# Paired heads in a cached-attention decode step, and a re-split of the last weight transfer

## The chip, the cores and the metric

The kernel runs on one core of one Trainium2 chip. Its five engines are TensorE (PE, matrix products), VectorE (DVE), ScalarE (ACT), GpSimd (POOL) and SyncE (SP, which here only issues DMAs). Sixteen DMA engines move data between device memory and the core's SBUF, whose 128 rows are called partitions. Matrix products land in PSUM, which DVE and ACT read. The metric is device time in microseconds of one execution, where smaller is better.

## The reference

One decode step for a batch of 4 tokens, model width 640, 32 heads of width 192. Attention looks at the last 2048 of 8192 cached positions. A gated feed-forward of width 1536 runs on the same normalised input, and the two results are added to the input.

```python
W = min(4096, max(256, Sk // 4))                 # 2048
q = (xn @ wq).reshape(B, Sq, Hq, Dh).transpose(0, 2, 1, 3)
scores = einsum("bhqd,bhkd->bhqk", q, k_cache[:, :, Sk - W:]) * Dh ** -0.5
o = einsum("bhqk,bhkd->bhqd", softmax(scores), v_cache[:, :, Sk - W:])
A = o.transpose(0, 2, 1, 3).reshape(B, Sq, Hq * Dh) @ wo
B = (silu(xn @ w1) * (xn @ w3)) @ w2
out = x + A + B                                   # xn = layernorm(x)
```

Nearly all bytes are the two caches: 32 heads x 3 MiB of keys and as much of values, all in bfloat16.

## The kernel before

A head's keys lie in SBUF as 128 partitions x 64 positions x 192: partition 4q+b holds 64 consecutive positions of batch row b. Values lie the same way, so no transposes of the caches are needed, and softmax over a batch row runs along 64 columns and across 32 partitions.

**Scores.** `mult` (L216) multiplies a chunk of `CH` = 16 positions of keys on DVE by the head's query, which `q_bcast` (L207) has spread over all partitions. `adder` (L225) sums the 192 products down to `DD` = 32 by six identity matmuls that accumulate in PSUM. `reduce_tile` (L233) sums those 32 on DVE. There are `NC` = 4 such steps per head, and 128 in all.

**Softmax.** `chain_lmax`, `chain_tr`, `chain_gmax`, `chain_bc` (L243 to L272) take each row's maximum: a DVE maximum, a PE transpose, a DVE maximum over 32 partitions, and a matmul that spreads it back. `chain_bc` then runs four exponentials on ACT per head, one for each batch row, each with a bias that sends the partitions of the other batch rows to zero. Their results are written straight into the columns of the weight tile `z`.

**Values.** `pv` (L281) multiplies `z` (32 columns, of which 8 are used: two positions x four batch rows) by two positions of values at a time: 32 matmuls of 384 columns per head, spread over four groups of PE columns. An ACT copy `o_sb` and `fold` (L297, a 32-bit selection matmul) gather the result. DVE scales it by the reciprocal row sum into `o_bf`. Every four heads `ge_tr` and `ge_proj` (L308, L315) transpose that and multiply by the output weights into `acc`.

**Tail.** `ffn_mm` (L338) forms the gate and up products, `ffn_transpose` (L356) turns their product around, and the loop at L417 multiplies by the down weights `w2`. Those are loaded in four transfers (L331): two whole thirds, three quarters of the last third, and its last quarter. The sum is added to `t1` and stored by two small DMAs.

**Order.** A table `sched` (L362 to L404) assigns every step a slot and a phase within it. One slot is one `mult`. Engines run their instructions in the order in which the steps are emitted, except where the Tile framework's scheduler reorders within the dependencies; `reduce_tile` is pinned on DVE behind the multiply `RLAG` slots ahead. All large loads are issued by SP in one order: keys of head h, values of head h-2, and so on. `kpool` and `vpool` hold three heads each, so keys of head h+3 wait until head h has been multiplied, and values of head h+3 until `pv` of head h is done. Eight DMA semaphores are used in turn, so a transfer is also issued no earlier than the landing of the one eight before it. The weights `w1`, `w3` and `w2` take over buffers of `kpool` at the end.

Of the kernel before, what the change touches and what calls it, by code (L numbers as in the profile page):

```python
# [18 lines left out]
def kernel(  # L19
# [12 lines left out]
    DD: int = 32,  # L32
    CH: int = 16,
    HG: int = 4,
    QP: int = 2,
    KBUFS: int = 3,
    VBUFS: int = 3,
    PBUFS: int = 4,
    NZ: int = 3,
    L: int = 9,  # L40
    RLAG: int = 2,
    ALIGN: int = 128,
):

# [3 lines left out]
    P = 128  # L48
# [12 lines left out]
    NS = H * NC  # L61
    RPP = (HG * Dh) // P
    QW = QP * Dh
    OW = HG * Dh
    NCH = 512
    FC = F // P
    DH = D // 2
    assert NJ % CH == 0 and CH * DD <= 512 and QW <= 512 and CH % 2 == 0
    assert (HG * Dh) % P == 0 and Dh % RPP == 0 and H % HG == 0 and HG % QP == 0
# [3 lines left out]
    NB = H // QP // NG  # L73
    assert H % (QP * NG) == 0 and NB <= 4
    assert DH <= 512 and F % NCH == 0 and NF <= NG and (NJ // 2) % NG == 0 and 2 * B <= 32
# [10 lines left out]
    ps_o = ctx.enter_context(tc.tile_pool(name="ps_o", bufs=2, space=MemoryType.PSUM))  # L86
# [4 lines left out]
    qbcs, wos, o_pss, rss, rcps, o_sbs, o_bfs, chs = ({} for _ in range(8))  # L91
    mult_insts = {}
# [5 lines left out]
    def load_k(h):  # L98
        kt = kpool.tile([P, NJ, Dh], BF16, tag="kt")
        nc.sync.dma_start(out=kt[:], in_=cache_rows(A_k_cache, h))  # L100
        kts[h] = kt

    def load_v(h):
        vt = vpool.tile([P, NJ, Dh], BF16, tag="vt")
        nc.sync.dma_start(out=vt[:], in_=cache_rows(A_v_cache, h))
        vts[h] = vt
# [6 lines left out]
    x_sb = const.tile([B, D], BF16, name="x_sb")  # L113
# [24 lines left out]
    ones_f = const.tile([P, 1 + ALIGN // 4], FP32, name="ones_f")[:, 0:1]  # L138
    nc.vector.memset(ones_f[:], 1.0)
    nsc = const.tile([1, B], FP32, name="nsc")  # L140
    nc.vector.memset(nsc[:], -SCALE)

    zs = []
    for i in range(NZ):
        z = const.tile([P, NJ // 2, 32], BF16, name=f"z{i}")
        nc.gpsimd.memset(z[:], 0.0)
        zs.append(z)
# [5 lines left out]
    rowsel = const.tile([P, 2 * B], FP32, name="rowsel")  # L153
    nc.vector.tensor_reduce(out=rowsel[:], in_=idf[:].rearrange("p (g c) -> p c g", g=NG)[:, 0:2 * B, :], axis=AX.X, op=ALU.add)
# [9 lines left out]
    sq = ppool.tile([B, D], FP32, tag="pr")  # L164
    ssq = const.tile([B, 1], FP32, name="ssq")
    nc.scalar.activation(out=sq[:], in_=xc[:], func=ACTF.Square, accum_out=ssq[:])
# [6 lines left out]
    xn = const.tile([B, D], BF16, name="xn")  # L173
# [10 lines left out]
    nc.vector.tensor_copy(out=sel[:], in_=rowsel[:, 0:B].unsqueeze(1).to_broadcast([P, NQ, B]))  # L184
    selT = ps_t.tile([P, B], FP32, tag="t")
    nc.tensor.matmul(selT[:], lhsT=sel[0:B].rearrange("k q b -> k (q b)"), rhs=idb[0:B, 0:B], start=True, stop=True)
    mbias = const.tile([P, B], FP32, name="mbias")
    nc.vector.tensor_scalar(out=mbias[:], in0=selT[:], scalar1=-1.0, scalar2=-MASK, op0=ALU.add, op1=ALU.mult)
# [4 lines left out]
    for k in range(NB):  # L193
        pool, tag = ((ps_add, "ps"), (ps_o, "o_ps"))[k // 2]
        qp = pool.tile([P, QW], FP32, tag=tag)
        q_pss.append(qp)
# [7 lines left out]
    for k in range(NB):  # L204
        nc.scalar.copy(out=q_sb[:, k, :], in_=q_pss[k][:])

    def q_bcast(qg):  # L207
        k, g = qg // NG, qg % NG
        bp = ps_t.tile([P, QW], FP32, tag="t")
        nc.tensor.matmul(bp[:], lhsT=sel[32 * g:32 * g + B].rearrange("k q b -> k (q b)"),  # L210
                         rhs=q_sb[32 * g:32 * g + B, k, :], start=True, stop=True)
        qbc = qpool.tile([P, QP, Dh], BF16, tag="qbc")
        nc.scalar.copy(out=qbc[:].rearrange("p h d -> p (h d)"), in_=bp[:])  # L213
        qbcs[qg] = qbc

    def mult(s):  # L216
        h, c = s // NC, s % NC
        pr = ppool.tile([P, CH, Dh], BF16, tag="pr")
        mi = nc.vector.tensor_tensor(out=pr[:], in0=kts[h][:, c * CH:(c + 1) * CH, :],  # L219
                                     in1=qbcs[h // QP][:, h % QP, :].unsqueeze(1).to_broadcast([P, CH, Dh]),  # L220
# [11 lines left out]

    def reduce_tile(s):  # L233
        h, c = s // NC, s % NC
        if c == 0:
            sc = small.tile([P, NJ], FP32, tag="sc", bufs=3)
            scs[h] = sc
        ri = nc.vector.tensor_reduce(out=scs[h][:, c * CH:(c + 1) * CH], in_=pss.pop(s)[:], axis=AX.X, op=ALU.add)  # L238
        ahead = min(s + RLAG, NS - 1)
        if ahead in mult_insts and ahead > s:  # L240
            tc.add_manual_dep(ri.ins, mult_insts[ahead].ins.name, ORDER_DEP, reason="vector engine issue order")

    def chain_lmax(h):  # L243
        lmax = small.tile([P, 1], FP32, tag="lmax")
        nc.vector.tensor_reduce(out=lmax[:], in_=scs[h][:], axis=AX.X, op=ALU.max)  # L245
        chs[h] = [lmax]

    def chain_tr(h):
        mt = ps_t.tile([P, P + B], FP32, tag="t")
        nc.tensor.transpose(out=mt[0:1, 0:P], in_=chs[h][0][:], identity=idf[:])  # L250
        chs[h].append(mt)

    def chain_gmax(h):
        gmax = small.tile([1, B], FP32, tag="gmax")
        nc.vector.tensor_reduce(out=gmax[:], in_=chs[h][1][0:1, 0:P].rearrange("o (q b) -> o b q", b=B),
                                axis=AX.X, op=ALU.max)
        gmq = small.tile([1, NQ, B], FP32, tag="gmq", bufs=1)
        nc.vector.tensor_copy(out=gmq[:], in_=gmax[:].unsqueeze(1).to_broadcast([1, NQ, B]))  # L258
        chs[h].append(gmq)

    def chain_bc(h):
        lmax, mt, gmq = chs.pop(h)
        sc = scs.pop(h)
        nc.tensor.matmul(mt[:, P:P + B], lhsT=gmq[:].rearrange("o q b -> o (q b)"), rhs=nsc[:], start=True, stop=True)  # L264
        negm = small.tile([P, B], FP32, tag="negm")
        nc.vector.tensor_tensor(out=negm[:], in0=mt[:, P:P + B], in1=mbias[:], op=ALU.add)  # L266
        z = zs[h % NZ][:].rearrange("p j (s b) -> p j s b", b=B)
        rs = small.tile([P, B], FP32, tag="rs")
        for b in range(B):
            nc.scalar.activation(out=z[:, :, 0:2, b], in_=sc[:].rearrange("p (j s) -> p j s", s=2), func=ACTF.Exp,  # L270
                                 bias=negm[:, b:b + 1], scale=SCALE, accum_out=rs[:, b:b + 1])
        rss[h] = rs  # L272

    def rowsum(h):
        tb = ps_t.tile([B, 1], FP32, tag="t")
        nc.tensor.matmul(tb[:], lhsT=rss.pop(h)[:], rhs=ones_f[:], start=True, stop=True)  # L276
        rcp = small.tile([B, 1], FP32, tag="rcp")
        nc.vector.reciprocal(out=rcp[:], in_=tb[:])  # L278
        rcps[h] = rcp

    def pv(s):  # L281
        h, c = s // NC, s % NC
        if c == 0:
            o_ps = ps_o.tile([P, 2 * Dh], FP32, tag="o_ps")
# [172 lines left out]
```

## Time and profile before

| | us |
|---|---|
| median of three runs | 529.87 (528.54 to 530.36) |
| the profiled execution: its own time | 528.51 |
| the profiled execution: its span | 526.6 |
| mean clock granted to TensorE in it | 0.853 of full |

In the profile, "busy" is the time an engine spent in instructions and "idle" names what it waited for. PEld is the loading of matmul weights, which overlaps PE. The DMA row gives the share of the sixteen engines' time that was spent moving packets. A completion of a DMA is written by each engine that took part in it, as a 4-byte packet behind its last data packet; the trace keeps the time, queue and size of each packet, but not the engine. Times within the execution are counted from the start of the span.

### The profile page before, as it was taken

Reading aid. Unit: us, or ns where it says so; the run is one execution under the profiler, and the core shown is the slowest. Engines: PE = TensorE matmul, PEld = TensorE weight load, DVE = VectorE, ACT = ScalarE, POOL = GpSimd, SP = SyncE. Lnnn points to the kernel's source line nnn. Section 1 sums busy time; section 2 is a strip of 40 time slices with the busy share of each in tenths; the row PEclk is TensorE's granted clock in tenths of the full one; section 3 lists DMA queues with packets and bytes.
Section 4 is the critical chain, followed back from the end, with each engine's and each line's share of the span. In section 5 each row is a group of like instructions: output and inputs, shape, how many; then the busy total and the mean of one; then the engine's idle time right before and its main releaser. Section 6 shows DMA issues by size and latency. Waiting matters only on the chain.

```text
span 526.6 us, 5872 instructions
## 1 busy us (share of the span) xinstructions
PE 360.0 (68%) x2384; PEld 148.4 (28%) x2384; DVE 340.2 (65%) x475; ACT 76.4 (15%) x318; POOL 4.5 (1%) x14
## 2 busy tenths in 40 slices
PE   1356767886676778767567976767678766668755
PEld 1122222332222333232222322223233322223322
DVE  4069766677666557777556677666567775665802
ACT  2101211101111111101111011111111011111130
POOL 3000000000000000000000000000000000000000
PEclk9999988778788887887878787888887887888888
DMA  8999999999999999999999999999999999999995
GB/s 359 439 425 437 429 429 431 432 424 435 437 429 435 429 434 429 433 432 431 429 433 428 426 440 426 437 429 431 432 433 431 429 436 430 431 426 440 423 426 218
DMA packets 11730, 223.33 MB, mean 424 GB/s; under 512 B 1316, under 2 KB 1464, under 8 KB 2872
## 3 DMA queue, kind: packets, MB, share of 16 engines
q1 hardware_dynamic: 11688, 222.97, 98.7%
q8 instruction: 18, 0.29, 0.2%
q14 instruction: 8, 0.07, 0.0%
q10 hardware_dynamic: 16, 0.01, 0.0%
HBM read 222.96 MB, written 0.01 MB: 423 GB/s over the span
## 4 chain that ended last, share of the span: by engine, by line
DMA 66%; DVE 21%; PE 9%; ACT 2%; issue 2%; SPq 0%; DVEq 0%; ACTq 0%
DMA kt<-in_A_k_cache_dram 61%; DVE pr L219 15%; PE ps L229 6%; DMA w2t<-in_B_w_dram 5%; DVE sc L238 5%; PE o_ps L289 1%; ACT z L270 1%; PE acc L321 1%; ACT o_sb L293 0%; DVE lmax L245 0%; SPq L129 0%; PE gp L312 0%; PE tb L276 0%; DVE rcp L278 0%; SPq L335 0%
## 5 line engine op out<-in xcount | busy, mean ns | idle before, releaser
L229 PE MATMUL ps<-pr,idb 128*128 128x512 bf16 x768 | 241.0, 470 | 110.4 <-DVE sc L238 101.1
L219 DVE TENSOR_TENSOR pr<-kt,qbc 128x3072 bf16<-128x3072 bf16 x128 | 223.3, 1745 | 35.5 <-DMA kt<-in_A_k_cache_dram 35.4
L229 PEld LDWEIGHTS <-idb 128*128 128x128 bf16 x768 | 85.3, 115 | 240.0 <-issue 190.4
L238 DVE TENSOR_REDUCE sc<-ps 128x16 f32<-128x512 f32 x128 | 86.9, 679 | 0.9 <-PE ps L229 0.9
L293 ACT COPY o_sb<-o_ps 128x384 f32<-128x384 f32 x32 | 15.1, 472 | 306.5 <-PE o_ps L289 306.5
L289 PE MATMUL o_ps<-vt,z 128*32 128x384 bf16 x1024 | 55.3, 334 | 3.8 <-DMA vt<-in_A_v_cache_dram 3.8
L270 ACT ACTIVATE z<-sc,negm 128x64 bf16<-128x64 f32 x128 | 45.7, 423 | 76.7 <-DVE negm L266 76.7
L266 DVE TENSOR_TENSOR negm<-mt,mbias 128x4 f32<-128x4 f32 x32 | 5.2, 161 | 70.7 <-PE mt L264 70.7
L306 DVE TENSOR_SCALAR o_bf<-fp,rcp 4x192 bf16<-4x192 f32 x32 | 12.9, 405 | 56.8 <-PE fp L302 29.9
L302 PE MATMUL fp<-o_sb,rowsel 128*4 128x192 f32 x128 | 26.7, 332 | 13.2 <-ACT o_sb L293 13.2
L289 PEld LDWEIGHTS <-z 128*32 128x32 bf16 x1024 | 25.0, 97 | 29.4 <-issue 20.8
L270 ACT ACTIVATION_READ_ACCUMULATOR z<-sc,negm 128x1 f32 x128 | 23.9, 187 | 0.0
L302 PEld LDWEIGHTS fp<-o_sb,rowsel 128*4 128x4 f32 x128 | 8.7, 87 | 24.2 <-ACT o_sb L293 18.6
L276 PE MATMUL tb<-ones_f,rs 128*4 128x1 f32 x64 | 6.2, 166 | 13.4 <-ACT z L270 13.4
L264 PE MATMUL mt<-nsc,gmq 1*128 1x4 f32 x64 | 12.2, 258 | 1.2 <-DVE gmq L258 1.2
L264 PEld LDWEIGHTS mt<-nsc,gmq 1*128 1x128 f32 x64 | 9.4, 183 | 12.1 <-issue 10.3
L276 PEld LDWEIGHTS tb<-ones_f,rs 128*4 128x4 f32 x64 | 3.6, 86 | 24.5 <-ACT z L270 23.0
L278 DVE RECIPROCAL rcp<-tb 4x1 f32<-4x1 f32 x32 | 4.9, 153 | 8.5 <-PE tb L276 8.5
L201 PE MATMUL qp<-wt,xnT 128*32 128x384 bf16 x80 | 7.0, 523 | 4.9 <-DMA wt<-in_A_wq_dram 4.9
L250 PE MATMUL mt<-idf,lmax 128*1 128x128 f32 x32 | 9.9, 308 | 0.5 <-DVE lmax L245 0.4
L321 PE MATMUL acc<-wt,oT 128*32 128x320 bf16 x96 | 9.7, 301 | 0.3 <-DVE oT L313 0.2
L213 ACT CAST qbc<-bp 128x384 bf16<-128x384 f32 x16 | 7.6, 485 | 7.7 <-PE bp L210 7.7
(61 smaller groups left out, 80.1 us busy)
## 6 DMA issues: line engine op xcount, KB each, us to landing
kt<-in_A_k_cache_dram SPq DMA_DIRECT2D x32, 3072.0 KB, 36.8
vt<-in_A_v_cache_dram SPq DMA_DIRECT2D x32, 3072.0 KB, 40.1
wt<-in_A_wo_dram SPq DMA_DIRECT2D x8, 960.0 KB, 36.5
wt<-in_A_wq_dram SPq DMA_DIRECT2D x2, 3072.0 KB, 13.2
wt<-in_B_w_dram SPq DMA_DIRECT2D x2, 1920.0 KB, 32.5
wt<-in_A_wq_dram SPq DMA_DIRECT2D x1, 1536.0 KB
w2t<-in_B_w_dram SPq DMA_DIRECT2D x2, 640.0 KB, 26.9
w2t<-in_B_w_dram SPq DMA_DIRECT2D x1, 480.0 KB, 27.6
```

The lines of the kernel that those rows point to most:

```text
L219: mi = nc.vector.tensor_tensor(out=pr[:], in0=kts[h][:, c * CH:(c + 1) * CH, :], in1=qbcs[h // QP][:, h % QP, :].unsqueeze(1).to_broadcast ...
L229: nc.tensor.matmul(ps[:], lhsT=idb[:], rhs=pr[:, :, kk * DD:(kk + 1) * DD], start=(kk == 0), stop=(kk == NK - 1))
L238: ri = nc.vector.tensor_reduce(out=scs[h][:, c * CH:(c + 1) * CH], in_=pss.pop(s)[:], axis=AX.X, op=ALU.add)
L250: nc.tensor.transpose(out=mt[0:1, 0:P], in_=chs[h][0][:], identity=idf[:])
L264: nc.tensor.matmul(mt[:, P:P + B], lhsT=gmq[:].rearrange("o q b -> o (q b)"), rhs=nsc[:], start=True, stop=True)
L270: nc.scalar.activation(out=z[:, :, 0:2, b], in_=sc[:].rearrange("p (j s) -> p j s", s=2), func=ACTF.Exp, bias=negm[:, b:b + 1], scale=SCAL ...
L276: nc.tensor.matmul(tb[:], lhsT=rss.pop(h)[:], rhs=ones_f[:], start=True, stop=True)
L289: nc.tensor.matmul(o_ps[32 * g:32 * g + 32, :], lhsT=z[:, jj, :], rhs=vt[:, 2 * jj:2 * jj + 2, :], start=(jj < NG), stop=(jj >= NJ // 2 - NG))
L293: nc.scalar.copy(out=o_sb[:].rearrange("r two d -> r (two d)"), in_=o_pss.pop(h)[:])
L302: nc.tensor.matmul(fp[:], lhsT=rowsel[:, two * B:(two + 1) * B], rhs=o_sb[:, two, :], start=(two == 0), stop=(two == 1))
L306: nc.vector.tensor_scalar_mul(out=o_bfs[hg][:, hl, :], in0=fp[:], scalar1=rcps.pop(h)[:, 0:1])
L321: nc.tensor.matmul(acc[32 * t:32 * t + 32, :], lhsT=oT[:, i, :], rhs=wo_t[:, i * D + t * DH:i * D + (t + 1) * DH], start=st, stop=sp)
```

## The change

The kernel works on two heads at a time (`HH` = 2) from the scores on, and on chunks of 32 positions (`CH` = 32, so `NC` = 2 steps per head; `DD` = 16, so twelve identity matmuls per step).

- The softmax chain runs once for two heads. One exponential per head, without masks, gives `e`; DVE multiplies it by the 0/1 mask `selb` into `z` (`chain_z`) for both heads.
- `pv` takes eight positions and 64 of the 192 value columns per matmul: 24 matmuls of 512 columns per head, on three groups of PE columns. Only the diagonal blocks of the result are wanted: `pick` multiplies by a 0/1 pattern on DVE, `pick_sum` adds up on DVE, `fold` gathers. PSUM output tiles are one pair deep (`ps_o` bufs 1) where there were two heads.
- The scaling by the reciprocal row sum moves from DVE to ACT, two calls per pair.
- Queries are projected in 60 matmuls of 512 columns (80 of 384 before), and broadcast in 12 pieces (16 before).
- In the schedule, values of head j are issued in the slot after head j's first multiply, and `pv` runs seven slots behind (a slot is now half a head).
- In the tail, the product of gate and up is formed twice: for all 512 columns, and once more (`hp`) for the columns of the last quarter of `w2`, in a permuted order. That quarter is loaded in two transfers (`w2_last`) of 64 partitions each, whose rows are read 8 by 8. `ffn_transpose` has a fifth transpose for it. The up product is now multiplied before `ge_tr`.

In the changed kernel PE runs the tail in this order: `pv` of the last head, `fold`, the up product, `ge_tr`, `ffn_transpose`, `ge_proj`, the down product. SP issues the same transfers in the same order as before, but for the first output weights, which go ahead of the fourth head's keys, and the two transfers in place of one at the end.

```diff
-    DD: int = 32,
-    CH: int = 16,
+    DD: int = 16,
+    CH: int = 32,
...
-    ps_o = ctx.enter_context(tc.tile_pool(name="ps_o", bufs=2, space=MemoryType.PSUM))
+    ps_o = ctx.enter_context(tc.tile_pool(name="ps_o", bufs=1, space=MemoryType.PSUM))
...
+        e = small.tile([P, HH, NJ], BF16, tag="e", bufs=2)
+        for hh in range(HH):
+            nc.scalar.activation(out=e[:, hh, :], in_=sc[:, hh, :], func=ACTF.Exp,
+                                 bias=negm[:, hh:hh + 1], scale=SCALE, accum_out=rs[:, hh:hh + 1])
...
+    def chain_z(u):
+        e = es.pop(u)
+        z = small.tile([P, HH, NJ, B], BF16, tag="z", bufs=2)
+        behind(nc.vector.tensor_tensor(out=z[:].rearrange("p h j b -> p (h j) b"),
+                                in0=e[:].rearrange("p h j -> p (h j)").unsqueeze(2).to_broadcast([P, HH * NJ, B]),
+                                in1=selb[:].unsqueeze(1).to_broadcast([P, HH * NJ, B]), op=ALU.mult))
...
+    def pv(j):
...
+        for g in range(GN):
+            for k in range(NV):
+                nc.tensor.matmul(o_ps[32 * k:32 * k + 32, hh, :],
+                                 lhsT=z[:, hh, g * PL:(g + 1) * PL, :].rearrange("p l b -> p (l b)"),
+                                 rhs=vt[:, g * PL:(g + 1) * PL, k * DV:(k + 1) * DV],
+                                 start=(g == 0), stop=(g == GN - 1))
+
+    def pick(u, h0, h1):
...
+        behind(nc.vector.tensor_tensor(out=o_ms[u][:, h0:h1].rearrange("r h l d -> r (h l) d"),
+                                       in0=o_pss[u][0:NV * 32, h0:h1, :].rearrange("r h (l d) -> r (h l) d", l=PL),
+                                       in1=diag[0:NV * 32, h0:h1, :].rearrange("r h l -> r (h l)").unsqueeze(2).to_broadcast([NV * 32, n, DV]), op=ALU.mult))
+
+    def pick_sum(u, h0, h1):
...
+        behind(nc.vector.tensor_reduce(out=o_rs[u][:, h0:h1, :], in_=o_ms[u][:, h0:h1].rearrange("r h l d -> r h d l"), axis=AX.X, op=ALU.add))
+
+    def fold(u):
...
+        for k in range(NV):
+            nc.tensor.matmul(fp[:, :, k * DV:(k + 1) * DV], lhsT=fsel[0:NV * 32, k, :], rhs=o_r[:], start=True, stop=True)
...
+        for hh in range(HH):
+            nc.scalar.mul(out=o_bfs[hg][:, pr + hh, :], in_=fp[:, hh, :], mul=rcp[:, hh:hh + 1])
...
+    def w2_last():
+        rows = B_w2[(NF - 1) * NCH:NF * NCH, :].rearrange("(h r s c) n -> h s r c n", h=2, r=8, s=8)
+        for h in range(2):
+            nc.sync.dma_start(out=ffn[2][64 * h:64 * h + 64, NF - 1, CF - 1, :], in_=rows[h, :, :, CF - 1, :])
...
+            nc.vector.tensor_tensor(out=hp[:].rearrange("m (h s r) -> m h s r", h=2, s=8), in0=last[0], in1=last[1], op=ALU.mult)
+            ffn["hp"] = hp
+            nc.vector.tensor_tensor(out=t_bf[0:32 * NF], in0=ffn["sg"][0:32 * NF], in1=t_bf[0:32 * NF], op=ALU.mult)
...
+        nc.tensor.transpose(out=hT_ps[:, CF * 32 * NF:], in_=ffn["hp"][:], identity=idb[0:32 * NF, 0:32 * NF])
...
+    PS = HH * NC
+    for j in range(H):
+        if j >= KBUFS:
+            add(NC * j - 3, 0, load_k, j)
+        add(NC * j + 2, 8, load_v, j)
+        add(NC * j + L, 2, pv, j)
...
+        add(PS * u + NC + L + 3, 2, fold, u)
...
+    add(end + 1, 0, w2_last)
...
+    add(end + 4, 0, ffn_mm, 1)
+    add(end + 9, 0, ffn_mm, 3)
+    add(end + 10, 0, ffn_transpose)
```

## The prediction

> **What bounds the kernel now.** I read the page's busy shares, its DMA rows, the stages of the tail with the share of the DMA engines, and the tail's instructions in order of time.
>
> ```profile
> PE 360.0 (68%) x2384; PEld 148.4 (28%) x2384; DVE 340.2 (65%) x475; ACT 76.4 (15%) x318; POOL 4.5 (1%) x14
> ...
> q1 hardware_dynamic: 11688, 222.97, 98.7%
> q8 instruction: 18, 0.29, 0.2%
> q14 instruction: 8, 0.07, 0.0%
> q10 hardware_dynamic: 16, 0.01, 0.0%
> ```
>
> The stages follow: from and to, length, busy time by engine, PE's clock, DMA share, GB/s.
>
> ```profile
> 400.00:480.00 80.00, 57.54 (x380) 23.48 (x381) 56.11 (x79) 10.23 (x47) 0.00 (x0) 0.84 1.01 432
> 517.00:518.00 1.00, 1.00 (x15) 0.31 (x9) 0.14 (x1) 0.00 (x0) 0.00 (x0) 1.00 0.98 405
> 518.00:519.00 1.00, 0.13 (x3) 0.00 (x0) 0.21 (x1) 0.58 (x1) 0.00 (x0) 1.00 0.82 332
> 519.00:520.00 1.00, 0.73 (x12) 0.57 (x14) 0.55 (x2) 0.00 (x0) 0.00 (x0) 1.00 0.64 264
> 520.00:521.00 1.00, 1.00 (x17) 0.67 (x13) 0.43 (x2) 0.00 (x0) 0.00 (x0) 1.00 0.56 229
> 521.00:522.00 1.00, 0.34 (x6) 0.22 (x5) 0.39 (x2) 0.00 (x0) 0.00 (x0) 1.00 0.31 118
> 522.00:523.00 1.00, 0.56 (x10) 0.29 (x6) 0.00 (x0) 0.00 (x0) 0.00 (x0) 1.00 0.10 40
> ```
>
> The load queue q1 fills 98.7% of the engines' span; in mid-run the share is 1.01, at 432 GB/s. No compute engine reaches 70%. A head's two loads take 2 x 7.27 us, the step between completions of successive 3 MiB transfers. What compute does before 500 us is free as long as loads stay queued. From 518 us the share falls in steps to 0.10: the sixteen DMA engines finish at different times, and the last decides.
>
> Why, the packet records tell. The sixteen completions of one transfer lie within 0.57 us at the start; those of the last values spread over 4.77. Each 16,384-byte packet of q8 (18 of them, 27.7 to 504.6 us) moves one engine's completions back by 1.42 us for good. They go round eight engines: the first, ninth and seventeenth hit the same one. These are instruction fetches, and PE's by their even 28 us step, for PE has 4768 of the 5872 instructions. Two engines get three, and these end last. The eight that q8 never hits include the four that carry four-row transfers (q10: 16 packets for two such, four data and four completions each).
>
> PE's part of the tail, in order of time:
>
> ```profile
> 511.86 2.75 PE L289 MATMUL o_ps<-vt,z 128*32 128x384 bf16 x32 [3.81 <-DMA vt<-in_A_v_cache_dram]
> 515.19 0.81 PE L302 MATMUL fp<-o_sb,rowsel 128*4 128x192 f32 x4 [0.58 <-ACT o_sb L293]
> 516.50 0.44 PE L312 MATMUL gp<-idb,o_bf 4*128 4x4 bf16 x6 [0.50 <-DVE o_bf L306]
> 516.87 1.26 PE L342 MATMUL gt<-wt,xnT 128*32 128x512 bf16 x15
> 519.27 0.36 PE L359 MATMUL hT_ps<-idb,hb 96*128 96x96 bf16 x4 [1.14 <-DVE hb L353]
> 519.55 0.99 PE L321 MATMUL acc<-wt,oT 128*32 128x320 bf16 x12
> 520.38 0.71 PE L420 MATMUL ff<-w2t,hT 128*32 128x320 bf16 x8
> 521.75 0.72 PE L420 MATMUL ff<-w2t,hT 128*32 128x320 bf16 x8 [0.66 <-DMA w2t<-in_B_w_dram]
> 522.91 0.72 PE L420 MATMUL ff<-w2t,hT 128*32 128x320 bf16 x8 [0.44 <-DMA w2t<-in_B_w_dram]
> ```
>
> See that the tail's first gate is the landing of the last values (511.69, PE from 511.86), that the last two groups of down products wait for transfers, and that the first group follows the output projection at once.
>
> **The change part by part.**
>
> *Main loop.* DVE: multiplies stay about 223 us (half as many, twice as long), the reductions L238 halve (64 x 0.679 = 43.5 for 86.9). Added are 16 masks (512 outputs), picks and pick sums (1024 inputs): at the rate of L238, 0.68 per 512 inputs, at most 16 x (0.7 + 1.4 + 1.4) = 56. So DVE stays near 340 us. ACT drops to 32 exponentials from 128. PE: 768 adders as before, 24 matmuls of 512 for 32 of 384 per head. Nothing on the path; the cover is the queue. Before, a values load is issued 40.1 us before it lands. Now it waits for `pv` three heads back, which PE reaches after the adders of the newest head, some 9 us after that head's keys land; V-2, K+1, V-1, K+2 and itself are then ahead, so it lands at 5 x 7.27 = 36 us after those keys. The stream runs dry only if the issue slips by a further 36 - 9 - 7 = 20 us. The keys behind it on SP slip too, within the same room.
>
> *Start.* Six small DVE reductions (L154: 0.185 each) ahead of `xnT`: +1.1 us; the first values load goes out at about 15 for 13.8. The queue holds until 40. Query pieces are ready near 26, and the first keys are used at 30.34: zero.
>
> *Instruction fetches.* PE's records by loop counts: 768 adders, 768 `pv`, 60 query, 96 `fold` (32-bit counts twice), 80 chain and row sum, 220 others: 1992 and as many loads, 3984 for 4768. One fetch per 4768/18 = 265 gives 15.0. Up to 16, no engine gets more than two: the slowest loses one delay, -1.42 us, from the 17th fetch's time (483.9 us) on. Bounds: 0 (if 17 or more are fetched) and -1.42; I take -1.42, the count leaving a margin of one. The landing of the last values moves to about 510.3.
>
> *Last quarter.* 8 packets per engine of 52 ns before: 0.42 us. Four rows went to four engines, so the 8-by-8 read may use 8 engines or all 16: bounds -0.42 and 0 for the engines hit by fetches; the others then take +0.42, and have about 1.7 us to spare. The Trainium skill ("DMA: Bandwidth & Descriptors", "Why a DMA increments its semaphore by 16 and not by 1") says that the largest divisor up to 16 of both patterns' slowest dimension sets the number of engines, the lowest-numbered ones: eight here. Its "Rules for kernel authors" speaks against the change: two transfers to partition halves are not worth it, as both use all 16 engines. By the one rule the landing gains 0.42 us, by the other nothing. My sum is the same either way, since PE ends later than that landing. One more issue on SP costs nothing: the four issues took 5.98 us from 494.39, and the fifth waits for the gate weights at about 503, some 15 us before its data is due.
>
> *Tail compute.* From the start of `pv` to the first down product it was 520.38 - 511.86 = 8.52. Now: `pv` 24 x 512/3 = 4096 column steps for 32 x 384/4 = 3072, at L289's 2.75 us (granted clock 0.5 there) 3.67; if the clock is full, 1.83. Pick 0.68 and sum 0.68 on DVE in place of the copy 0.48; with waits `fold` starts at 5.15 (3.33 before) and takes 0.81. The up product follows at once: 1.26, cast 0.66, `hp` 0.25 (between L154's 0.19 and L353's 0.42), product 0.42, five transposes 0.5, output projection 0.95: 10.1 in all, or 8.3 at full clock. The ACT scalings (2 x 0.4, nearest L306's 0.405) hide beside the up product's 1.26. From 510.44 the first down product comes at 520.5 (518.7), and three groups of 0.72 end at 522.7. By DMA: three quarters land at 522.82 - 1.42 = 521.4, eight products after that end at 522.3. Before, the last product ended at 523.63.
>
> *Sum.* -0.95 with `pv` at half clock, -1.35 at full clock, where the landing holds it. The clock of that 3.4 us stretch depends on PE's idle stretch before it, so I take -1.2: 528.5 - 1.2 = 527.3 for the profiled execution. The median of the runs is 1.36 above that execution, so I forecast 529.87 - 1.2 = **528.7**.
>
> **The rivals.**
>
> *No gain.* PE still fetches 17 times, or DMA engines not hit by q8 hold the end. Then `pv` starts at 511.86, and the longer tail (10.1) puts the first down product at 522.0 and the last at 524.1: +0.5, or 0 at full clock: 529.9 to 530.4. For it: the count is an estimate. Against it: 15 is two short of 17.
>
> *More.* The runs scatter by 1.8 us and their median is 1.36 above the profiled execution. If that excess is the same stagger of DMA engines, part goes too: -1.2 - 1.3 = -2.5, 527.4. For it: nothing else of the stream varies in mid-run. Against it: the stagger of one execution is all that is seen.
>
> *Slower.* With one pair of output buffers, `pv` of the next pair waits for `pick` on DVE behind a multiply that waits for keys, and PE, whose adders free the two product buffers, stands with it. PE needs 360/32 = 11.25 us of a head's 14.54, so it decides once this stall passes 6.6 us per pair; each us beyond costs 16 us, 2 us give 562. Against it: `pick` is emitted a slot ahead, and costs 1.4.
>
> **How the numbers follow.** Forecast 0.58, no gain 0.10, more 0.24, slower 0.08. A measurement of this kernel tells a difference from no change at about 0.3%, 1.6 us. The forecast lies within that, but somewhat under half of it would be measured beyond, with runs that scatter by 0.9 to each side: faster 0.26 + 0.24 = 0.50; same 0.32 + 0.10 = 0.42; slower 0.08. The range goes from the gaining rival to the one without gain, 527.3 to 530.2; the slower one lies outside.
>
> **What would show it.** Right: q8 with 15 packets (14 to 16); share 1.0 in mid-run; the last `pv` starting near 510.4; the step-down from 518 us shorter; the last down products no longer waiting for a transfer, or by under 0.3 us. Wrong: 17 or more packets of q8; a mid-run share under 0.98; PE waiting on `pick` by microseconds; `pv` to the first down product over 10.5 us.

## The result

The changed kernel takes **527.44 us** (median of 7 runs, 527.27 to 527.97), the kernel before, run beside it, 529.34 (528.35 to 531.14). The ratio is 0.9965, with a 95% interval of 0.9948 to 0.9982. Two later comparisons of the same two programs gave 0.9974 (0.9963 to 0.9985) and 0.9967 (0.9954 to 0.9979). So the change gains 1.7 to 1.9 us, where 1.2 was forecast; 527.44 is inside the range (527.3 to 530.2) and on its lower edge.

The profiled execution took 527.86 us, with a span of 526.0 and a mean granted clock of 0.814. Its page, busy time and DMA queues:

```profile
PE 331.0 (63%) x1992; PEld 143.6 (27%) x1992; DVE 328.2 (62%) x290; ACT 39.5 (8%) x121; POOL 1.8 (0%) x11
...
q1 hardware_dynamic: 11688, 222.97, 98.8%
q8 instruction: 15, 0.25, 0.2%
q14 instruction: 4, 0.03, 0.0%
```

Two numbers of q8 and q1 matter. The instruction fetches (the packets of q8) are 15, as counted. The packets of q1 are 11688 as before, although there is one transfer more. Each engine that takes part in a transfer writes a completion packet, so one transfer on 16 engines (16 completions) has become two on 8 engines each (2 x 8): the 8-by-8 read uses eight engines.

The stages (from and to, length, busy time by engine, PE's granted clock, DMA share, GB/s):

```profile
400.00:480.00 80.00, 56.41 (x335) 25.10 (x334) 54.50 (x45) 3.68 (x14) 0.00 (x0) 0.83 1.00 431
...
517.00:518.00 1.00, 0.38 (x8) 0.29 (x6) 0.45 (x2) 0.58 (x1) 0.00 (x0) 0.50 1.01 419
518.00:519.00 1.00, 0.40 (x5) 0.38 (x5) 0.51 (x2) 0.00 (x0) 0.00 (x0) 0.50 0.92 357
519.00:520.00 1.00, 1.00 (x11) 0.54 (x10) 0.41 (x1) 0.00 (x0) 0.00 (x0) 0.50 0.55 200
520.00:521.00 1.00, 1.00 (x12) 0.54 (x10) 0.05 (x1) 0.00 (x0) 0.00 (x0) 0.50 0.50 197
521.00:522.00 1.00, 1.00 (x10) 0.57 (x8) 0.75 (x2) 0.00 (x0) 0.00 (x0) 0.50 0.12 45
522.00:523.00 1.00, 1.00 (x16) 0.60 (x12) 0.00 (x0) 0.00 (x0) 0.00 (x0) 0.99 0.00 0
```

Mid-run is as full as it was (1.00, 431 GB/s). The staircase at the end has lost its last step: the share reaches zero after 522, where 0.10 was left before. Read the clock column too: TensorE has half its clock from 515.2 to 522.0.

PE's part of the tail, in order of time:

```profile
510.51 1.91 PE L313 MATMUL o_ps<-vt,z 128*32 128x512 bf16 x24 [0.36 <-DMA vt<-in_A_v_cache_dram]
514.25 0.82 PE L338 MATMUL fp<-o_r,fsel 96*4 96x128 f32 x6 [1.83 <-DVE o_r L331]
514.92 2.09 PE L386 MATMUL gt<-wt,xnT 128*32 128x512 bf16 x15
516.94 0.44 PE L350 MATMUL gp<-idb,o_bf 4*128 4x4 bf16 x6
518.60 0.51 PE L408 MATMUL hT_ps<-idb,t_bf 96*128 96x96 bf16 x4 [1.22 <-DVE t_bf L401]
518.91 0.28 PE L409 MATMUL hT_ps<-idb,hp 96*128 96x96 bf16 x1
519.12 1.78 PE L357 MATMUL acc<-wt,oT 128*32 128x320 bf16 x12
520.69 2.45 PE L482 MATMUL ft<-w2t,hT 128*32 128x320 bf16 x24
```

`pv` of the last head starts 1.35 us sooner (510.51 for 511.86). In this execution the 24 down products run without a wait for a transfer and end at 523.14. Behind the down products stand only the last sum on DVE and the two stores.

From the packet records: the completions of the last values lie within 3.14 us (4.77 before), and the last down weights land at 521.77 (523.00 before). This execution has half the clock in the tail; the next one profiled has full clock there, and in it the last eight down products do wait for their transfer (below).

### The profile page after: what moved, and what is told of

The parts are those of the page before. It is cut to its first block, busy times and chain, and to the rows that moved or that the text cites. A ratio compares the mean times of both kernels' runs of the same rounds, so it can differ in the third digit from the quotient of the medians.

```text
span 526.0 us, 4662 instructions
## 1 busy us (share of the span) xinstructions
PE 331.0 (63%) x1992; PEld 143.6 (27%) x1992; DVE 328.2 (62%) x290; ACT 39.5 (8%) x121; POOL 1.8 (0%) x11
## 3 DMA queue, kind: packets, MB, share of 16 engines
q1 hardware_dynamic: 11688, 222.97, 98.8%
## 4 chain that ended last, share of the span: by engine, by line
DMA 76%; DVE 14%; PE 9%; SPq 1%; issue 0%; ACT 0%; DVEq 0%; ACTq 0%
DMA kt<-in_A_k_cache_dram 72%; DVE pr L228 12%; PE ps L238 5%; DMA vt<-in_A_v_cache_dram 3%; PE o_ps L313 2%; DVE sc L253 1%; PE acc L357 1%; DVE o_r L331 0%; PE ft L482 0%; PE gt L386 0%; DVE o_m L323 0%; SPq L112 0%; SPq L136 0%; PE fp L338 0%; DVE z L291 0%
## 5 line engine op out<-in xcount | busy, mean ns | idle before, releaser
L238 PE MATMUL ps<-pr,idb 128*128 128x512 bf16 x768 | 226.5, 457 | 162.9 <-DVE pr L228 162.9
L228 DVE TENSOR_TENSOR pr<-kt,qbc 128x6144 bf16<-128x6144 bf16 x64 | 214.5, 3352 | 164.7 <-DMA kt<-in_A_k_cache_dram 164.7
L313 PE MATMUL o_ps<-vt,z 128*32 128x512 bf16 x768 | 66.5, 390 | 0.9 <-DVE z L291 0.5
L253 DVE TENSOR_REDUCE sc<-ps 128x32 f32<-128x512 f32 x64 | 43.7, 682 | 9.8 <-PE ps L238 9.8
L313 PEld LDWEIGHTS <-z 128*32 128x32 bf16 x768 | 32.1, 98 | 28.3 <-issue 10.8
L331 DVE TENSOR_REDUCE o_r<-o_m 96x128 f32<-96x1024 f32 (+1 forms) x17 | 30.6, 1800 | 0.1
L283 ACT ACTIVATE e<-sc,negm 128x64 bf16<-128x64 f32 x32 | 10.9, 340 | 238.5 <-DVE negm L279 238.5
L323 DVE TENSOR_TENSOR o_m<-o_ps,diag 96x1024 f32<-96x1024 f32 (+1 forms) x17 | 19.5, 1148 | 7.4 <-PE o_ps L313 7.4
L344 ACT ACTIVATE o_bf<-fp,rcp 4x192 bf16<-4x192 f32 x32 | 11.4, 403 | 133.1 <-PE fp L338 133.1
L338 PE MATMUL fp<-o_r,fsel 96*4 96x128 f32 x96 | 13.1, 273 | 1.8 <-DVE o_r L331 1.8
L291 DVE TENSOR_TENSOR z<-e,selb 128x512 bf16<-128x512 bf16 x16 | 10.8, 678 | 0.9 <-ACT e L283 0.9
```

Of the source, the lines that this page charges most:

```text
L228: mi = nc.vector.tensor_tensor(out=pr[:], in0=kts[j][:, c * CH:(c + 1) * CH, :], in1=qbcs[j // QP][:, j % QP, :].unsqueeze(1).to_broadcast ...
L238: nc.tensor.matmul(ps[:], lhsT=idb[:], rhs=pr[:, :, kk * DD:(kk + 1) * DD], start=(kk == 0), stop=(kk == NK - 1))
L253: ri = nc.vector.tensor_reduce(out=scs[j // HH][:, j % HH, c * CH:(c + 1) * CH], in_=pss.pop(s)[:], axis=AX.X, op=ALU.add)
L283: nc.scalar.activation(out=e[:, hh, :], in_=sc[:, hh, :], func=ACTF.Exp, bias=negm[:, hh:hh + 1], scale=SCALE, accum_out=rs[:, hh:hh + 1])
L291: behind(nc.vector.tensor_tensor(out=z[:].rearrange("p h j b -> p (h j) b"), in0=e[:].rearrange("p h j -> p (h j)").unsqueeze(2).to_broadc ...
L313: nc.tensor.matmul(o_ps[32 * k:32 * k + 32, hh, :], lhsT=z[:, hh, g * PL:(g + 1) * PL, :].rearrange("p l b -> p (l b)"), rhs=vt[:, g * PL: ...
```

## Experiments

Three questions were open. Does the fetch count move the end, in steps of eight? What does the split of the last quarter do? And why is the gain of the medians (1.9) larger than that of the two profiled executions (528.51 - 527.86 = 0.65)?

### The fetches

The changed kernel unaltered, and the same with idle products put ahead of the row sums, whose results nothing reads:

```diff
-        tb = ps_t.tile([B, HH], FP32, tag="t")
-        nc.tensor.matmul(tb[:], lhsT=selm[:], rhs=rss.pop(u)[:], start=True, stop=True)
+        tb = ps_t.tile([B, HH + B], FP32, tag="t")
+        for _ in range(30 if u < H // HH - 1 else 0):        # 82, and 76, in the other two
+            nc.tensor.matmul(tb[:, HH:], lhsT=selb[:], rhs=selb[:], start=True, stop=True)
+        nc.tensor.matmul(tb[:, 0:HH], lhsT=selm[:], rhs=rss.pop(u)[:], start=True, stop=True)
```

The changed kernel again:

> The changed kernel, unchanged, as the base for the runs beside it and for a second profile of its tail. Its median of 7 runs was 527.44 us (527.27 to 527.97). Expected: 527.4, a q8 row of 15 packets again, and the down products again without a wait for a transfer. If PE's clock is at full in the tail here (it was granted 0.5 from 515 to 522 us in the first profile), the last products end 1 us or so earlier, but not before the landing of the last weights (521.8 in the first profile).

With 30 such products per pair of heads:

> The changed kernel with 900 added PE instructions (30 tiny products with 30 loads in each of the first 15 pairs, results unused), so that PE's stream is as long as that of the kernel before. Theory (instruction fetches stagger the DMA engines, and the most-hit one decides): q8 shows 18 packets, two engines get a third fetch, the last values land 1.4 us later and the end moves by 1.4 us: 528.8. Rival A (PE's own time or instruction count matters): the end moves in proportion to the added instructions. Rival B (fetches do not matter): 527.4.

With 82:

> The same with 2460 added PE instructions (82 products with 82 loads in each of the first 15 pairs). Theory: q8 shows 24 packets, which is three for each of the eight engines, so that the most-hit engine has as many as with 18: also 1.4 us over the changed kernel, 528.8, no more than with 900. Rival A (in proportion): 2.7 times the loss of the run with 900, 3.8 us if that is 1.4. Rival B: 527.4, unless PE itself falls behind the stream (its busy time would rise from 331 to about 395 us of 526, which is within what the stream allows).

And later, with 76, since 82 had given one fetch more than wanted:

> The changed kernel with 76 more 4-column matmuls ahead of each row sum but the last: 6264 PE instructions, by one fetch per 256 of them exactly 24 fetches, three for each of the eight DMA engines. Theory A (steps): only the third fetch on the slowest engine counts, so this costs no more than the run with 19 fetches did: 529.0 to 529.5, the spread of the last completions near 4.5 us. Theory B (each fetch costs): 9 fetches more than 15 at the loss of 0.4 us each that 19 showed (1.55 / 4): 531. Theory C (the run with 25 fetches was slow by PE's extra instructions and not by a fourth delay): as that run, 530.8.

Measured, in order of the fetches (PE instructions are matmuls plus weight loads; a DMA engine's largest share follows from fetches going round eight engines):

| | PE instructions | fetches (q8) | most on one engine | last down weights land | median us |
|---|---|---|---|---|---|
| changed | 3984 | 15 | 2 | 521.99 | 527.58 (527.36 to 527.95) |
| before | 4768 | 18 | 3 | 523.00 | 529.25 (528.15 to 531.35) |
| + 30 | 4884 | 19 | 3 | 523.17 | 529.13 (528.76 to 530.45) |
| + 76 | 6264 | 24 | 3 | 523.12 | 528.96 (528.76 to 530.73) |
| + 82 | 6444 | 25 | 4 | 524.37 | 530.85 (530.07 to 532.05) |

The run with 76 stands beside a changed kernel at 527.48, the others in the table beside the one at 527.58. The queue of the run with 24 fetches, and its PE tail:

```profile
PE 360.5 (68%) x3132; PEld 173.2 (33%) x3132; DVE 328.7 (62%) x290; ACT 39.6 (8%) x121; POOL 1.8 (0%) x11
...
q8 instruction: 24, 0.39, 0.3%
```

```profile
511.89 1.93 PE L315 MATMUL o_ps<-vt,z 128*32 128x512 bf16 x24
...
520.60 0.72 PE L484 MATMUL ft<-w2t,hT 128*32 128x320 bf16 x8
522.22 0.72 PE L484 MATMUL ft<-w2t,hT 128*32 128x320 bf16 x8 [0.90 <-DMA w2t<-in_B_w_dram]
523.38 0.72 PE L484 MATMUL ft<-w2t,hT 128*32 128x320 bf16 x8 [0.44 <-DMA w2t<-in_B_w_dram]
```

See that PE does 30 us more than in the changed kernel and the time is still that of the run with 19 fetches: PE's work is covered, and five further fetches cost nothing while they fall on engines with two. The 25th, at 516.0 us, gives one engine a fourth. The last landing then comes 1.25 us later, and the time stands 3.27 us above the changed kernel beside it, where the run with 24 stands 1.48 above its own: 1.8 more. The step theory holds; that each fetch costs, and that the extra PE instructions were to blame, both fall.

One rule fits all five counts: one fetch per 256 PE instructions, rounded down (4884/256 = 19.1, 6264/256 = 24.5). The prediction had divided by 265, which is why the run meant for 18 got 19, and that meant for 24 got 25.

From 15 to 19 fetches costs 529.13 - 527.58 = 1.55 us, and from 15 to 24 costs 528.96 - 527.48 = 1.48. With 19 the changed kernel is as long as the kernel before (0.9998, interval 0.9985 to 1.0012). So in the median the three fetches that it saves are worth its whole gain, and everything else in the change nets to nothing that these runs resolve. The scatter is not the same, though: eleven of the twelve spans with 19 fetches lie between 527.0 and 527.5, where those of the kernel before lie at 526.3 to 526.9 or well above (below). No run took fetches out of the kernel before.

The expectation for the changed kernel's second run missed on one point. Its tail had full clock (from 510.1 to 523.7), and its last eight down products waited 0.42 us for their weights, which landed at 521.99. So with full clock the transfers still end this kernel, and with half the clock PE's chain does.

### The last quarter of the down weights

First the split was undone outright, with `hp`, its transpose and the wider `hT` gone:

```diff
-        nc.tensor.transpose(out=hT_ps[:, CF * 32 * NF:], in_=ffn["hp"][:], identity=idb[0:32 * NF, 0:32 * NF])
...
-    hT = const.tile([P, (CF + 1) * 32 * NF], BF16, name="hT")
+    hT = const.tile([P, CF * 32 * NF], BF16, name="hT")
...
-        add(end + 1, 0, w2_load, n, 0, CF if n < NF - 1 else CF - 1)
-    add(end + 1, 0, w2_last)
+        for c0, c1 in ((0, CF),) if n < NF - 1 else ((0, CF - 1), (CF - 1, CF)):
+            add(end + 1, 0, w2_load, n, c0, c1)
```

> The changed kernel with the last quarter of the down weights in one transfer of 128 partitions again, and without the second product and the fifth transpose. Theory (PE's chain behind the last values ends later than any landing): the last landing comes up to 0.42 us later, 522.2 for 521.8, still a microsecond before PE is done (523.1), and PE saves 0.4 us of the second product: time within 0.4 us of the changed kernel, either way. Rival (the last landing is the end): 0.4 us slower. Second rival (the transfer on eight engines costs its own doubling): 0.4 us faster because of the landing.

It took 529.92 us (529.7 to 530.65), 2.3 more than the changed kernel beside it: no expectation allowed for that. The loss lies in mid-run, where the edit does nothing: packets of 24,576 bytes took 914 ns in the median and 916.9 in the mean, for 912 and 913.1, and by 490 us the stream was 2.4 us behind (209 MB had been moved at 490.39, for 487.99). What the edit also did is move every later buffer down by 448 bytes: the first key buffer went from byte 24320 of a partition (a multiple of 256) to 23872 (64 past one), by the tile sizes in the kernel. Two runs separate the two. One undoes the split but keeps both tiles, so that addresses stay:

```diff
-            nc.vector.tensor_tensor(out=hp[:].rearrange("m (h s r) -> m h s r", h=2, s=8), in0=last[0], in1=last[1], op=ALU.mult)
+            nc.vector.memset(hp[:, 0:1], 0.0)
...
-        nc.tensor.transpose(out=hT_ps[:, CF * 32 * NF:], in_=ffn["hp"][:], identity=idb[0:32 * NF, 0:32 * NF])
-        nc.vector.tensor_copy(out=hT[:], in_=hT_ps[:])
+        nc.vector.tensor_copy(out=hT[:, 0:CF * 32 * NF], in_=hT_ps[:, 0:CF * 32 * NF])
```

> The changed kernel with the last quarter in one transfer of 128 partitions, without the second product and the fifth transpose, but with the tiles for both still allocated, so that no buffer's address moves (the kernel that left them out had its key and value buffers at 64 bytes past a multiple of 256, and its 24,576-byte packets took 914 ns instead of 912 in mid-run). Theory (addresses made the loss of 2.3 us there, the split itself is worth little): packets of 912 ns again and 527.2 to 527.8, within 0.4 us of the changed kernel. Rival (the split is worth 2 us or more): 529.9 again.

The other keeps the changed kernel and moves the buffers by 64 bytes alone, to 24384:

```diff
-    ALIGN: int = 208,
+    ALIGN: int = 272,
```

> The changed kernel with 64 bytes more of padding ahead of its large buffers and nothing else: key and value buffers start 64 bytes past a multiple of 256, where they started on one. Theory (a start off the 256-byte grid slows every large packet): packets of 914 ns and more in mid-run, and 2 us lost: 529.6. Rival (padding does not matter, the loss came from the tail): 527.5.

With the addresses moved: 530.34 us (530.26 to 530.67), again 914 and 916.9 ns. With the split undone and the addresses kept: **527.09** (526.9 to 527.67), at 912 ns. So the address cost some 2.8 us in both runs that moved it (against 527.1 and 527.5, measured apart from them), and the split itself seems to cost rather than help. The second was run again, beside the changed kernel:

> The changed kernel with the last quarter of the down weights as one transfer again and all buffers at their addresses, a second time, beside the changed kernel itself. Theory A: the split costs time in this kernel, by its extra multiply, its fifth transpose and its second issue ahead of the first down product: this run is 0.3 to 0.6 us below the changed kernel beside it (527.1 was measured for it before, 527.4 and 527.6 for the changed kernel). Theory B: that difference was scatter between calls: the two agree within 0.2 us.

> The changed kernel once more, beside the run with one transfer. Theory A: 527.4 to 527.6; theory B: within 0.2 us of the run with one transfer.

527.09 (526.95 to 527.76) against 527.48 (527.31 to 528.12): by the medians the split costs 0.39 us. The ranges overlap, since four of the ten runs with one transfer took 527.66 or more; the means differ by 0.22. In these two traces the clocks differ too. First DVE with one transfer, then with two (start, length):

```profile
517.32 0.17 DVE L351 COPY oT<-gp 128x24 bf16<-128x24 bf16 x1 [2.36 <-PE gp L350]
517.64 0.42 DVE L398 TENSOR_TENSOR t_bf<-sg,t_bf 96x512 bf16<-96x512 bf16 x1
518.51 0.36 DVE L406 COPY hT<-hT_ps 128x384 bf16<-128x384 bf16 x1 [0.45 <-PE hT_ps L405]
```

```profile
517.43 0.17 DVE L351 COPY oT<-gp 128x24 bf16<-128x24 bf16 x1 [3.07 <-PE gp L350]
517.73 0.37 DVE L399 TENSOR_TENSOR hp<-sg,t_bf 96x128 bf16<-96x128 bf16 x1
518.14 0.42 DVE L401 TENSOR_TENSOR t_bf<-sg,t_bf 96x512 bf16<-96x512 bf16 x1
519.24 0.41 DVE L410 COPY hT<-hT_ps 128x480 bf16<-128x480 bf16 x1 [0.68 <-PE hT_ps L409]
```

`hp` takes 0.37 us and stands ahead of the product that every transpose waits for. Whether that moves the end depends on the clock. The changed kernel's second run and the one above with one transfer both had full clock in the tail (510.1 to 523.7, and 509.8 to 523.5). Their down products, first with two transfers, then with one:

```profile
519.81 1.58 PE L482 MATMUL ft<-w2t,hT 128*32 128x320 bf16 x16
521.81 0.97 PE L482 MATMUL ft<-w2t,hT 128*32 128x320 bf16 x8 [0.42 <-DMA w2t<-in_B_w_dram]
```

```profile
519.23 0.71 PE L478 MATMUL ft<-w2t,hT 128*32 128x320 bf16 x8
520.55 0.72 PE L478 MATMUL ft<-w2t,hT 128*32 128x320 bf16 x8 [0.61 <-DMA w2t<-in_B_w_dram]
521.68 0.72 PE L478 MATMUL ft<-w2t,hT 128*32 128x320 bf16 x8 [0.41 <-DMA w2t<-in_B_w_dram]
```

They end at 522.78 and 522.40; the other run with one transfer, at full clock too, ends at 522.36. So the split costs 0.38 to 0.42 us here, and `hp` is not the reason: the later start of the first product is taken up by the wait. The last weights land at 521.99 with two transfers and at 521.78 and 521.73 with one, and the products end 0.79 us after that for 0.62 and 0.63; why they do is open. With half the clock nothing waits for the last weights, and `hp` stands in the chain; no pair of profiles shows its cost there.

The transfers don't pay for `hp`. The packets of the last quarter are of 1,280 bytes and follow each other every 52 ns; those of the three quarters before it are of 3,840. In four executions with one transfer, two of each kernel, the last 3,840-byte packet ends 0.42 us before the last data: eight small packets follow it on the engine that ends last. With two transfers eight engines carry sixteen small packets each, 0.84 us, and the other eight none, and these are not the eight of the fetches. In the changed kernel's first profile five engines without small packets end between 521.06 and 521.22; two with sixteen have their last 3,840-byte packets behind them at 520.82 and 520.92 and end at 521.66 and 521.76. So the split relieves the engine that would have ended last, at an estimated 521.22 + 0.42 = 521.64, and doubles the share of others that would have ended only some 0.3 us earlier. The same estimate for the other two profiles gives 521.80 and 521.97 with one transfer, where 521.99 and 521.98 were seen with two: a loss of 0.01 to 0.19 us. The landings agree: 521.74 and 521.78 with one transfer, and 521.77, 521.98 and 521.99 with two, later by 0.15 in the mean.

The kernel before with the split alone, its extra tiles put where nothing else moves:

```diff
-        for c0, c1 in ((0, CF),) if n < NF - 1 else ((0, CF - 1), (CF - 1, CF)):
-            add(end, 0, w2_load, n, c0, c1)
+        add(end, 0, w2_load, n, 0, CF if n < NF - 1 else CF - 1)
+    add(end, 0, w2_last)
...
+        nc.tensor.transpose(out=hT_ps[:, CF, :], in_=ffn["hp"][:], identity=idb[0:32 * NF, 0:32 * NF])
```

> The kernel before with the split of the last quarter alone: two transfers of 64 partitions, 8 by 8, from permuted rows, with the extra multiply and transpose, other buffers at their addresses. Theory A: the transfers leave the eight DMA engines that the fetches hit, as the completion counts show in the changed kernel; the last landing comes up to 0.42 us sooner, but the multiply and transpose add some 0.4 us ahead of the first down product: between -0.4 and +0.2 us against the kernel before. Theory B: the two transfers use the engines that end last and 0.42 us more lies on them: +0.4 us, the last landing at 523.5 instead of 523.1.

529.04 us (528.68 to 531.57) beside 529.22, ratio 1.0007 (0.999 to 1.0023): in the time the two theories can't be told apart, since this kernel scatters too widely. In the landing they can: 523.33, for 523.00 and 523.08 without the split, and the last 3,840-byte packet ends 0.84 us before it, for 0.42. That is the second theory's mechanism, with 0.3 of its 0.42 us: in this kernel the two engines with three fetches both carry sixteen small packets.

### The scatter of the kernel before

> The kernel before, unchanged, for a second profile and for how its times scatter: in 35 runs it took 528.15 to 531.35 us, in clusters near 528.3, 529.3, 530.3 and 531, where the changed kernel takes 527.36 to 527.95. Theory (instruction fetches land on different DMA engines from run to run, and the tail waits for the slowest): a run of another cluster shows another engine, or the same with more hits, ending last, with mid-run packets of 912 ns. Rival (another DMA rate in mid-run): mid-run packets longer than 912 ns in the slower runs.

529.94 us (528.33 to 531.12). This time the profiled execution was a long one: 530.01, span 528.2. Its last weights landed at 523.08 (523.00 in the first profile), with the same 18 fetches and a spread of 4.82 (4.77). So the DMA engines end alike in the short execution and in the long one, and a varying stagger of theirs is not the cause. PE's tail in it:

```profile
511.91 2.75 PE L289 MATMUL o_ps<-vt,z 128*32 128x384 bf16 x32 [5.33 <-DMA vt<-in_A_v_cache_dram]
515.24 1.44 PE L302 MATMUL fp<-o_sb,rowsel 128*4 128x192 f32 x4 [0.58 <-ACT o_sb L293]
517.54 2.32 PE L342 MATMUL gt<-wt,xnT 128*32 128x512 bf16 x15
521.44 1.78 PE L321 MATMUL acc<-wt,oT 128*32 128x320 bf16 x12
523.02 2.24 PE L420 MATMUL ff<-w2t,hT 128*32 128x320 bf16 x24
```

The clock column of its stages:

```profile
511.00:514.00 3.00, 2.09 (x28) 1.21 (x31) 0.00 (x0) 0.00 (x0) 0.00 (x0) 0.50 0.99 421
514.00:517.00 3.00, 2.10 (x15) 0.35 (x4) 0.28 (x1) 0.48 (x1) 0.00 (x0) 0.50 0.97 405
517.00:520.00 3.00, 2.69 (x21) 0.96 (x21) 0.29 (x2) 0.09 (x1) 0.00 (x0) 0.50 0.82 337
520.00:523.00 3.00, 2.00 (x16) 1.17 (x18) 0.78 (x2) 0.49 (x1) 0.00 (x0) 0.50 0.33 133
```

The work and the landing are the same; the granted clock is 0.50 from 510.3 to 523.9, where the first profile had full clock from 515.0 to 525.3. `fold` takes 1.44 for 0.81, the up product 2.32 for 1.26, the projection 1.78 for 0.99, and the last product ends at 525.26 for 523.63. The changed kernel's chain, at half clock from 515.2, ends at 523.14. With full clock in both tails it is 522.78 (the changed kernel again) against 523.63. A third execution of the changed kernel took 528.12, so the gain between single profiled executions is anything from 0.39 (528.51 - 528.12) to 2.55 us (530.01 - 527.46), by which clock each of them got. The profile of the kernel before with the split, another long execution (530.31, span 528.5), agrees: its clock is at half from 510.8 to 524.5 and its last product ends at 525.60.

The runs agree. Of 102 runs of the kernel before, 50 have spans of 526.3 to 526.9, 18 of 527.0 to 527.5, and 34 of 528.0 to 529.5; all 24 later runs of the changed kernel lie between 525.5 and 526.3. The mean falls by 1.78 us (529.35 to 527.57), of which 1.58 is span. The other 0.20 is time outside the span: 15 of the 102 have 2.36 to 3.22 us of it, the 24 never more than 1.86. What that is, and the spans above 528.5, no profile here caught; nor does a profile of the changed kernel have half the clock through its whole tail.

### The last values ahead of the gate weights

An attempt at a better version: the last values are issued before the gate weights, whose product moves behind the last head.

```diff
-    add(end - 2, 9, ffn_load, 1)
+    add(end, 9, ffn_load, 1)
...
-    add(end + 4, 0, ffn_mm, 1)
-    add(end + 9, 0, ffn_mm, 3)
-    add(end + 10, 0, ffn_transpose)
+    add(end + 9, 3, ffn_mm, 1)
+    add(end + 10, 0, ffn_mm, 3)
+    add(end + 10, 1, ffn_transpose)
```

> The changed kernel with the last head's values issued ahead of the gate weights, and the gate product moved behind that head's work on PE. Theory (in the changed kernel PE's chain behind the last values ends it, and the landing of the last weights is 0.5 to 1 us earlier): the chain starts 4.6 us earlier and hides; the end is then the last landing plus some 0.8 us of products: 0.4 to 0.9 us faster, 526.8. Rival (the transfers end it already): the same, 527.5.

528.63 us (528.03 to 530.38), 1.1 worse than the changed kernel's 527.5 in the other comparisons. The profile is of one of its long executions (530.16; seven of the twelve took 528.71 or less):

```profile
509.33 1.91 PE L313 MATMUL o_ps<-vt,z 128*32 128x512 bf16 x24 [0.78 <-DVE o_m L323]
513.06 0.82 PE L338 MATMUL fp<-o_r,fsel 96*4 96x128 f32 x6 [1.82 <-DVE o_r L331]
514.69 0.43 PE L350 MATMUL gp<-idb,o_bf 4*128 4x4 bf16 x6 [0.81 <-ACT o_bf L344]
515.05 4.04 PE L386 MATMUL gt<-wt,xnT 128*32 128x512 bf16 x30
```

Two new things stand in the way of the gain; that they do so in the shorter executions as well is not shown. `pv` no longer waits for its values but for `pick` of the head before (0.78 <-DVE o_m), the wait that the single pair of output buffers makes. And the gate product, which used to run while PE waited, is now in the chain: 4.04 us for both products, partly at half clock. Besides, the last down weights landed only at 524.12. Between 495 and 505 us the stream moved 403 and 405 GB/s, where the changed kernel moved 434 and 431. What slowed it there stays open.

## Why the prediction was right, and where not

- **Instruction fetches: right.** 15 were foretold and seen, one landing delay of 1.42 was the term, and the runs with more fetches price it at 1.48 to 1.55. Last values foretold for about 510.3, `pv` for 510.4: it started at 510.51. The margin to the 17th fetch was larger than told: by one per 256 the 17th needs 4352 instructions, 368 more. The last weights land only 1.01 to 1.23 us sooner (521.77 to 521.99 for 523.00), the split among the reasons. *No gain* fell with the 15 fetches; where 19 bring its condition about, the time is 529.13 and not 529.9 to 530.4.
- **Main loop: right.** DVE 328 us (340 foretold; pick sums take 1.90 us each for 1.4, but picks 1.21 for 1.4, and the multiplies 214.5 in all for 223), share 1.00, 431 GB/s. Values land 37.0 us after their issue in the median; the prediction's 36 us counted from the keys, 9 us before the issue, so it had 27, and the loads stay queued for longer than it said. The stall behind *Slower* did not come: of the idle time before the weight loads of `pv`, the profile puts 10.8 us down to issue, 1.4 to `z` and 1.0 to values, and none to `pick`.
- **Last quarter: wrong.** The step bounded the landing by -0.42 and 0 for the engines that the fetches hit and let "the others then take +0.42", with "about 1.7 us to spare". It took the eight engines of the transfers to be ones that no fetch hits. Some are hit: engines with two fetches took +0.42 us of packets and end last, +0.01 to +0.19 by the estimate above and +0.15 in the measured mean (+0.3 in the kernel before). The sum held `hp`'s 0.25 and took the landing as indifferent; at full clock the landing decides, and the split costs 0.38 to 0.42.
- **Tail compute: right in sum by luck, wrong in its terms.** 10.1 us from `pv` to the first down product if half a clock falls in it, and 8.3 if not: 510.51 to 520.69 is 10.18, and in the execution with full clock 511.10 to 519.81 is 8.71. But the half clock fell on the up product (2.09 for 1.26) and the projection (1.78 for 0.95), not on `pv` (1.91); the pick sum took 1.01 for 0.68, `hp` 0.37 for 0.25. The sign that the last products wait for a transfer by under 0.3 us held in two profiles and failed in the one with full clock (0.42).
- **Sum for the profiled execution: too hopeful.** 527.3 foretold; 527.46, 527.86 and 528.12 measured in three executions, so 0.39 to 1.05 us below the 528.51 before, where 1.2 was forecast.
- **From it to the median: the step that failed.** "The median of the runs is 1.36 above that execution" was carried over unchanged, to 528.7. The excess was the kernel before's own: its profile had shown one of its shortest executions, and a third of its runs have spans at least 1.4 us longer. In the two long executions that were profiled, one of them with the split, TensorE's clock is at half through the tail, and in the kernel before the work and the landings of the tail are those of the short one. The changed kernel's medians (527.44 to 527.58) lie within 0.7 us of its profiled executions. Of the 1.26 us between 528.7 and 527.44, 0.53 is the base (529.87 from three runs, 529.34 from the seven beside the changed kernel), and 0.73 is the gain, 1.9 for 1.2. That the range held is thus partly luck: the sum for one execution was too low, and the step to the median too high by more.
- ***More* gave the number (527.4) by a mechanism that is not there:** the stagger of the DMA engines is the same in short and long executions of the kernel before. Its condition, that the excess goes, held: at half clock the changed kernel's products end 0.36 and 0.64 us later than at full clock (523.14 and 523.42 for 522.78), where those of the kernel before end 1.63 later (525.26 for 523.63). Its half clock covers 6.8 us of the tail, though, and that of the kernel before 13.6; why the changed kernel's spans don't spread further is not shown.

The Trainium skill's two rules ("DMA: Bandwidth & Descriptors") split the verdict. "Why a DMA increments its semaphore by 16 and not by 1" gives this read eight engines, and the unchanged 11688 packets agree; which eight, the trace doesn't name. "Rules for kernel authors" says that two transfers to partition halves spray over all 16, which doesn't hold for this read, by these packets; its advice, one transfer over 128 partitions, is borne out by 0.39 us (527.09 for 527.48, `hp` and the fifth transpose included).

## What to carry to other kernels

In a kernel that the DMA engines bound, count PE's instructions in steps: here each fetch costs one of eight engines 1.42 us, and what counts is how many the worst engine gets, so that 784 instructions less were worth 1.5 us and five fetches more were worth nothing. Put a split of the last transfer on paper engine by engine before building it: it helps only if it takes bytes off the engine that ends last without adding as many to one that ends a little earlier, as it did here; with one transfer and the same addresses the kernel takes 527.09 us, the fastest of all versions run. And read the granted clock in the tail of a long and a short execution before explaining scatter by anything else.

## What was not expected of the hardware

- **Addresses.** Moving the key and value buffers from a multiple of 256 bytes to 64 past one made the same 24,576-byte packets take 916.9 ns instead of 913.1 in the mean. Each engine moves 512 of them, so that is 1.95 us; the kernel lost 2.8, and where the rest went is open. No other offset was tried. An experiment that deletes a small tile can thus cost more than the thing it tests. The Trainium skill ("DMA: Bandwidth & Descriptors", "How a descriptor splits into AXI transactions") counts extra beats for a descriptor that doesn't start at a multiple of 256 bytes; these two runs agree in direction, though here it is the destination that moved.
- **Fetches.** One 16,384-byte packet per 256 PE instructions, in turn on eight of the sixteen engines, in all five counts from 15 to 25.
- **Clock.** With the same program and the same landings, TensorE had half its clock for 13.6 us of the tail in one execution and full clock from 515 us on in another, and the chain ended 1.6 us apart.
